# Windowed attention and a residual MLP on one core: copying three sets of transposes with one PSUM bank per engine, and three steps moved

## The chip, the cores and the metric

The kernel runs on one core of a Trainium2 chip. The metric is the time of one execution on the device in microseconds (us). The core's engines are TensorE (PE, with its weight loads listed apart as PEld), VectorE (DVE), ScalarE (ACT), GpSimd (POOL) and SyncE (SP); SP, ACT and POOL also issue DMAs. All times in this document are from profiled executions or from timed runs of the kernels shown.

## What is computed

Two parts, one after the other. First attention with a sliding window of 128 keys and 4 sink keys, for 4 batches, 8 heads, 768 positions, head size 64. Its heads side by side are the rows `x` (4 x 768 x 512) of a residual MLP that mixes first over positions and then over channels:

```python
scores = scale * np.matmul(q, k.transpose(0, 1, 3, 2))
scores = np.where(is_sink | in_window, scores, -1e9)
x = softmax(scores) @ v                       # heads side by side: B, S, 512
a1 = alpha1 * x + beta1
u  = x + lam * np.einsum('ts,bsd->btd', w_tok, a1)
a2 = alpha2 * u + beta2
out = u + lam * (np.maximum(a2 @ w_ch1, 0) @ w_ch2)   # 512 -> 2048 -> 512
```

## The kernel before

**Stages.** The four batches go through the stages below, one batch's MLP interleaved with the next batch's attention.

- q and k are cast to 16 bits and transposed on TensorE (`tp`, L505); scores are made for a block j of 128 keys and two groups of four heads (`S`, tiles `Sb_j_G`, L608), exponentials on ACT (`E`, L630), and masked by a multiplication on DVE (L645; on some blocks on POOL, L570). The sink keys have a small matmul of their own (`sk`, L540) and an exponential (`es`, L545). `pv` (L709) multiplies by v; DVE divides by the sums (L734, L735); POOL or DVE apply the first affine (`xh`, L753, L756).
- Token mixing: `tok` (L840), six matmuls of 128x512 for a block `ti` of 128 positions. DVE adds the result to x, which gives u (`ua`, L847), and ACT or POOL cast u to 16 bits (`u16`, L157 on POOL, L155 on ACT, both by the helper `copy`).
- u's transposes: for a half `chk` of 384 positions TensorE transposes three blocks `u16` of four groups of 128 channels (L881). Two channel groups go into one tile `uTp`, which is one bank of PSUM; so a set (a batch and a half) has two banks, `uTpb_chk_0` and `uTpb_chk_1`, with two channel groups each. Each channel group is copied to `uT` with the second affine by one instruction of 128x384, on ACT (L864) or on DVE (L866).
- First channel layer: `h` (L901), four matmuls of 128x384 for one of 16 channel blocks `fi` of a half, and a relu to `hT` on ACT (L907) or DVE (L909).
- Second channel layer: in batch 0 plain (`ch`, L1086, added to x by DVE at L1097); in batches 1 to 3 by Strassen's seven products `P1` to `P7` (`P`, L1018, eight matmuls of 128x256 for a block nt). P3 is added up in the bank of P5. Sums of w2 (`w2s`, and w2f in place, L933, on DVE or POOL) and of hT (L959 to L962) are made ahead. DVE adds the products to x (L1031) and into a side tile `pt` (L1049), and `pt` is added to x by DVE or POOL (L1054, L1057).

**Names.** `h1_0_13` is the tile h of batch 1, half 0, channel block 13; `tok1_5` the token mixing of batch 1, block 5; `u16_1_4` the cast of u of batch 1, block 4; `S2_1` the scores of batch 2, key block 1, both groups; `x3_5` the rows of batch 3, block 5; `P5_2_1` the product P5 of batch 2, nt 1.

**What sets the order.** Nothing is decided on the chip. The program makes 1153 tasks (a task is a few instructions of one engine), and a list written out by hand, `ORDER`, says in which order they are issued; the string `ENGINES` says which engine does each task, `HOMES` which buffer each tile takes. Each engine runs its own tasks in the order of that list. Between engines the framework adds semaphores. Four banks of PSUM hold all tiles of the kind "d" in turn (`tok`, `uTp`, `h`, `P`, `ch`, `pv`, `sk`, `tp`), so a tile's first matmul waits until the bank's former tile was read. The framework also makes two engines that touch one bank wait for each other: in the program's semaphores, an L866 on DVE waits for the L864 on ACT that reads the other half of the same bank, or the other way round.

**Around the change.** In batch 1's first set, each bank is copied by both engines; TensorE's order there is the two banks of transposes, four matmuls of `ch0_4`, `tok1_3` (in the bank of uTp1_0_1), `tok1_5` (in the bank of ch0_4), `tok1_4`, four matmuls of `pv2_0_0`, `h1_0_0`, `h1_0_2`, S2_1, then the second set's two banks, `h1_0_1`, `h1_0_13` (in the bank of uTp1_1_1), `h1_0_14` (in that of uTp1_1_0), `h1_0_15`. The copies of DVE stand among the subtraction of w2 (L933), the add of ch0_4 (L1097), the mask of E2_0_0 (L645) and the three adds of tok1_3, tok1_5 and tok1_4 (L847). The casts `u16_1_5` and `u16_1_4` are on POOL, `u16_1_3` on ACT. In batch 3, TensorE's order is tok3_5, P5_2_2, P3_2_0 (in the bank of P5_2_0), P5_2_1 (in the bank of tok3_5), the second set's banks uTp3_1_1 (in the bank of P5_2_0) and uTp3_1_0, P3_2_2, `h3_0_13` (in the bank of uTp3_1_1), `h3_0_1` (in the bank of uTp3_1_0), P3_2_1 (in the bank of P5_2_1), h3_0_12.

These lines issue a set's transposes and copies (`affine` holds L864 and L866):

```python
a = add(p, {PE: 336}, tr, [done["u16", b, 3 * chk + i] for i in range(3)], [pt] + us)
for ci in range(2):
    c = 2 * cp + ci
    done["uT", b, chk, c] = add(
        p + 0.1 + 0.01 * ci, {DVE: 395, ACT: 575},
        lambda e, ci=ci, c=c: affine(
            e, bo.t[:, c, chk * NTOK : (chk + 1) * NTOK], pt.t[:, ci, :], c),
        [a, done["ab2"]], [pt, bo])
```

Of the kernel before, what the change touches and what calls it, by code (L numbers as in the profile page):

```python
# [77 lines left out]
def kernel(  # L78
# [119 lines left out]
    for r in range(NR):  # L198
# [43 lines left out]
        451, 440, 452, 639, 453, 417, 319, 640, 309, 648, 446, 649, 320, 447, 418, 323, 321,  # L242
        448, 645, 664, 646, 324, 322, 449, 623, 329, 650, 665, 454, 347, 325, 651, 455, 330,
        652, 348, 326, 462, 456, 463, 464, 459, 656, 457, 327, 458, 659, 627, 460, 657, 662,
        625, 461, 331, 38, 629, 468, 356, 465, 470, 469, 332, 343, 466, 630, 467, 471, 660,
        333, 350, 622, 328, 310, 661, 658, 477, 884, 342, 883, 472, 474, 473, 889, 478, 479,
        671, 486, 475, 490, 476, 487, 344, 666, 491, 663, 483, 480, 484, 485, 488, 482, 481,
        672, 512, 489, 514, 513, 886, 669, 516, 515, 496, 667, 670, 506, 354, 497, 500, 517,
        507, 346, 510, 668, 684, 511, 881, 677, 685, 502, 678, 501, 682, 504, 683, 546, 505,
        686, 524, 503, 547, 334, 680, 520, 916, 525, 526, 687, 521, 628, 910, 544, 527, 631,  # L250
# [20 lines left out]
        807, 814, 990, 808, 841, 991, 987, 988, 839, 989, 842, 992, 845, 840, 843, 846, 822,  # L271
        847, 844, 993, 849, 836, 994, 850, 821, 997, 995, 848, 1000, 835, 998, 855, 1001,
        999, 851, 837, 996, 1002, 859, 838, 1012, 852, 856, 853, 860, 1006, 1013, 1009,
        1007, 1008, 1014, 1003, 863, 1004, 1005, 854, 1015, 1010, 864, 1011, 857, 872, 862,
        869, 1016, 873, 1017, 866, 870, 861, 1021, 1018, 1022, 1023, 878, 858, 1019, 1020,
        1050, 867, 879, 1026, 875, 1027, 1051, 1048, 876, 1030, 1049, 1038, 1031, 1042,
        1039, 1028, 1043, 1034, 1029, 1044, 1052, 1045, 1035, 1046, 1086, 1047, 1053, 1080,
        1087, 1084, 874, 1081, 1064, 1085, 1032, 1065, 1070, 1033, 1068, 1071, 1058, 1024,
# [11 lines left out]
        "4444433134433334413334413314444042210221021021020121321021320202020020211212020202020212"  # L290
        "1212020212120202120212120212121202020202022221022221422221022221422221022221013111111331"
        "1111333333302002002132132002032002102020101212010321213120301212131201012121312010121213"
        "1203212131212131213213210201201210213213201201212020202120202121212020202021212020212121"
        "2120211120202120202020201120212121212111112121212121212113211121312142102142142142104444"
        "0000444044333333020020320020020020020020020201012120101212133201012121312030121213120101"
        "2121332032121312121312102102102012012102102102012012121212021212121212120212120202120212"
        "1202020202011212020202021202011202121212121111121212121212121312111213121021421421021421"
        "4044440440440443333330200200200200203200203200202010121203012121312010121213320103212131"
        "2030121213120321213321213121021021020120121021321320120120202120212021212021202020202021"
        "2020212120202020112020212021202020112120210202142141111212121212121211121112131210210214"  # L300
        "214214210"
    )
# [993 lines left out]
```

## Time and profile before

| | us |
|---|---|
| median of 3 runs (267.78 to 268.67) | 268.48 |
| the profiled execution | 268.26 |
| its span, first to last instruction | 266.3 |
| PE busy | 257.6 |
| DVE busy | 196.0 |
| ACT busy | 140.0 |
| POOL busy | 113.2 |

The granted TensorE clock is full in every slice of the page. The span is the profiled execution without what lies before the first and after the last instruction. Matmuls are pipelined, and a row of the timeline gives the start and the length until the modelled end of the last one, which can lie past the start of the next row. In a row of the timeline the brackets hold the engine's idle time before it and what ended that time.

### The profile page before, as it was taken

The numbers are of one execution on the slowest core, as the hardware profiler recorded it, in microseconds if no ns is written. First come the engines' busy times: TensorE is split into PE (matmuls) and PEld (weight loads), VectorE is DVE, ScalarE is ACT, GpSimd is POOL, SyncE is SP. The second block draws the span as 40 slices with busy tenths as digits, with TensorE's granted clock in tenths as the row PEclk, the third lists the DMA queues.
The fourth block names the chain that finished last, engine by engine and source line by source line (L and its number), as shares of the span: only waits on it lengthen the run. The fifth ranks groups of instructions, "written<-read, shape, count | busy, mean of one in ns | idle before, by whom it ended". The sixth has DMA issues, their size and how long they took to land.

```text
span 266.3 us, 5785 instructions
## 1 busy us (share of the span) xinstructions
PE 257.6 (97%) x2335; PEld 170.8 (64%) x2335; DVE 196.0 (74%) x403; ACT 140.0 (53%) x227; POOL 113.2 (43%) x131
## 2 busy tenths in 40 slices
PE   8999999999999999999999999999999999999993
PEld 8755556675556544565787776667667666667882
DVE  5789898679787748687877976588688974128892
ACT  1389744799967434669773452752760324543000
POOL 7826906979974437134763030064563120000010
PEclk9999999999999999999999999999999999999999
DMA  7999999999186307637430007010000000100217
GB/s 214 212 273 326 231 249 354 369 268 315 44 214 206 79 0 190 186 100 196 86 118 2 0 0 238 2 42 0 2 0 2 0 2 0 39 2 1 98 68 269
DMA packets 43058, 33.30 MB, mean 125 GB/s; under 512 B 26372, under 2 KB 37388, under 8 KB 43032
## 3 DMA queue, kind: packets, MB, share of 16 engines
q1 hardware_dynamic: 31728, 23.34, 29.6%
q10 hardware_dynamic: 7560, 6.32, 7.8%
q0 software_dynamic: 3744, 3.28, 7.7%
q8 instruction: 18, 0.29, 0.5%
q14 instruction: 8, 0.07, 0.1%
HBM read 29.91 MB, written 6.29 MB: 136 GB/s over the span
## 4 chain that ended last, share of the span: by engine, by line
PE 81%; DVE 8%; ACT 5%; DMA 2%; issue 1%; SPq 0%; DVEq 0%; ACTq 0%
PE h L901 29%; PE P L1018 19%; PE tok L840 9%; PE ch L1086 8%; PE pv L709 3%; PE tp L505 3%; PE S L608 3%; PE idle L148 3%; DMA nat<-in_q_dram 2%; ACT uT L864 2%; DVE uT L866 1%; ACT E L630 1%; PE uTp L881 1%; DVE qkT L157 1%; DVE x L735 1%
## 5 line engine op out<-in xcount | busy, mean ns | idle before, releaser
L901 PE MATMUL h<-uT,w1f 128*128 128x384 f16 x512 | 90.4, 326 | 1.1 <-DVE uT L866 0.5
L901 PEld LDWEIGHTS <-w1f 128*128 128x128 f16 x512 | 48.0, 98 | 32.8 <-issue 3.6
L907 ACT ACTIVATE hT<-h 128x384 f16<-128x384 f32 x77 | 36.2, 492 | 35.1 <-PE h L901 29.5
L909 DVE TENSOR_SCALAR hT<-h 128x384 f16<-128x384 f32 x51 | 27.8, 554 | 22.0 <-PE h L901 19.6
L1018 PEld LDWEIGHTS <-hT 128*128 128x128 f16 x408 | 39.3, 98 | 7.3 <-issue 1.0
L630 ACT ACTIVATE E<-S 128x1024 f16<-128x1024 f32 (+1 forms) x39 | 38.2, 1002 | 6.4 <-PE S L608 4.9
L753 POOL TENSOR_TENSOR tm<-x,la_b 128x512 f32<-128x512 f32 x18 | 24.4, 1358 | 28.1 <-DVE x L735 14.7
L840 PE MATMUL tok<-xh,wtokT 128*128 128x512 f16 x144 | 33.3, 379 | 0.3 <-DVE x L1097 0.2
L1018 PE MATMUL P<-w2f,hT 128*128 128x256 f16 x216 | 26.9, 273 | 0.0
L155 ACT COPY qkT<-tp 128x768 f16<-128x768 f16 x24 | 19.0, 800 | 11.8 <-PE tp L505 11.1
L1031 DVE TENSOR_TENSOR x<-x,P 128x256 f32<-128x256 f32 x45 | 18.2, 418 | 9.2 <-PE P L1018 8.8
L1018 PE MATMUL P<-w2s,hT 128*128 128x256 f16 x192 | 23.7, 273 | 0.5 <-DVE x L847 0.4
L155 ACT CAST u<-x 128x512 f16<-128x512 f32 x16 | 9.6, 618 | 27.7 <-DVE x L847 27.3
L840 PEld LDWEIGHTS <-wtokT 128*128 128x128 f16 x144 | 13.8, 97 | 15.5 <-issue 1.1
L1086 PE MATMUL ch<-w2f,hT 128*128 128x512 f16 x96 | 23.4, 380 | 0.0
L1054 POOL TENSOR_TENSOR x<-x,pt 128x256 f32<-128x256 f32 x4 | 3.4, 853 | 46.5 <-DVE pt L1049 46.5
L735 DVE TENSOR_TENSOR x<-pv,rec 128x256 f32<-128x256 f32 x48 | 20.4, 425 | 1.7
L847 DVE TENSOR_TENSOR x<-x,tok 128x512 f32<-128x512 f32 x24 | 16.0, 682 | 4.4 <-PE tok L840 4.1
L709 PEld LDWEIGHTS <-E 128*128 128x128 f16 x328 | 14.9, 97 | 4.9 <-issue 1.1
L709 PE MATMUL pv<-vfs,E 128*128 128x65 f16 x328 | 17.6, 194 | 0.0
L822 POOL TENSOR_TENSOR w2f<-wst_w,lam_b 128x512 f16<-128x512 f32 x12 | 16.9, 1431 | 0.0
L864 ACT ACTIVATE uT<-uTp,ab 128x384 f16<-128x384 f16 x16 | 10.2, 668 | 11.8 <-PE uTp L881 9.7
(131 smaller groups left out, 376.0 us busy)
## 6 DMA issues: line engine op xcount, KB each, us to landing
wst_w<-in_moe_w_ch_dram SPq DMA_DIRECT2D x8, 512.0 KB, 7.1
nat<-in_q_dram SPq DMA_DIRECT2D x10, 384.0 KB, 6.9
nat<-in_k_dram SPq DMA_DIRECT2D x10, 384.0 KB, 5.6
vnat<-in_v_dram SPq DMA_DIRECT2D x14, 256.0 KB, 4.7
out_dram<-x SPq DMA_DIRECT2D x11, 256.0 KB, 2.4
out_dram<-x ACTq DMA_DIRECT2D x10, 256.0 KB, 2.1
wtn<-in_moe_w_tok_dram SPq DMA_DIRECT2D x6, 384.0 KB, 5.9
w1f<-in_moe_w_ch_dram POOLq DMA_DIRECT2D x4, 512.0 KB, 10.5
```

The lines of the kernel that those rows point to most:

```text
L155: nc.scalar.copy(o, i)
L630: nc.scalar.activation(eT.t, pS.t[:, :, 0 : n * w].rearrange("p e (i w) -> p e i w", i=n), AF.Exp, scale=scale)
L709: nc.tensor.matmul(po.t[:, hl, :], eT.t[:, e_, off + i, c : c + P], vf[j][:, h, :], start=(r < 2 and n == 0), stop=(n == len(parts) - 1 an ...
L735: nc.vector.tensor_mul(bx.t[:, 4 * G : 4 * G + 4, :], po.t[:, :, 0:D], rec.t.to_broadcast([P, 4, D]))
L753: engine[e].tensor_mul(bt.t, bx.t.rearrange("p h d -> p (h d)"), la1_b)
L840: nc.tensor.matmul(pt.t, wtokT[:, si, ti * P : (ti + 1) * P], hs[si].t, start=(si == 0), stop=(si == NR - 1))
L901: nc.tensor.matmul(ph.t, w1f[:, c, fi * P : (fi + 1) * P], bu.t[:, c, chk * NTOK : (chk + 1) * NTOK], start=(c == 0), stop=(c == NC - 1))
L907: nc.scalar.activation(bh.t[:, fi, :], ph.t, AF.Relu)
L909: nc.vector.tensor_scalar_max(bh.t[:, fi, :], ph.t, 0.0)
L1018: nc.tensor.matmul(pc.t, hh[:, nt * P : (nt + 1) * P], w(fi), start=(first and n_ == 0), stop=(n_ == HF - 1), skip_group_check=True)
L1031: nc.vector.tensor_add(row(bx)[:, cols], row(bx)[:, cols], pc.t)
L1086: nc.tensor.matmul(pc.t, bh.t[:, fi, nt * P : (nt + 1) * P], w2f[:, fi, :], start=(fi == 0), stop=(fi == NF - 1))
```

## The change

The order of the tasks and the engines of four of them are changed; no instruction is added or taken away, and no tile gets another buffer.

- Engines: in batch 1's first set, both copies of bank uTp1_0_1 are DVE's and both of uTp1_0_0 ACT's (before: one of each on each engine). In batch 1's second set, uTp1_1_1 is ACT's and uTp1_1_0 DVE's. In batch 3's second set, uTp3_1_1 is DVE's and uTp3_1_0 ACT's. Each engine has as many copies as before.
- Task 666, the scores S2_1 on TensorE, moves from before the transposes of batch 1's second set to behind them and behind h1_0_1.
- Task 1016, the add L847 of x3_5 on DVE, moves ahead of task 862, the add L1057 of x2_5.
- Task 333, the add L1097 of x0_4 on DVE, moves ahead of task 467 (a copy that was DVE's and is now ACT's) and of 471 (tok1_3).

```diff
-        625, 461, 331, 38, 629, 468, 356, 465, 470, 469, 332, 343, 466, 630, 467, 471, 660,
-        333, 350, 622, 328, 310, 661, 658, 477, 884, 342, 883, 472, 474, 473, 889, 478, 479,
-        671, 486, 475, 490, 476, 487, 344, 666, 491, 663, 483, 480, 484, 485, 488, 482, 481,
+        625, 461, 331, 38, 629, 468, 356, 465, 470, 469, 332, 343, 466, 630, 333, 467, 471,
+        660, 350, 622, 328, 310, 661, 658, 477, 884, 342, 883, 472, 474, 473, 889, 478, 479,
+        671, 486, 475, 490, 476, 487, 344, 491, 663, 483, 480, 484, 485, 488, 666, 482, 481,
...
-        1007, 1008, 1014, 1003, 863, 1004, 1005, 854, 1015, 1010, 864, 1011, 857, 872, 862,
-        869, 1016, 873, 1017, 866, 870, 861, 1021, 1018, 1022, 1023, 878, 858, 1019, 1020,
+        1007, 1008, 1014, 1003, 863, 1004, 1005, 854, 1015, 1010, 864, 1011, 857, 872, 1016,
+        862, 869, 873, 1017, 866, 870, 861, 1021, 1018, 1022, 1023, 878, 858, 1019, 1020,
...
-        "1203212131212131213213210201201210213213201201212020202120202121212020202021212020212121"
+        "1203212131212131213213210200211210213213211200212020202120202121212020202021212020212121"
...
-        "2030121213120321213321213121021021020120121021321320120120202120212021212021202020202021"
+        "2030121213120321213321213121021021020120121021321320021120202120212021212021202020202021"
```

In `ENGINES` a 0 is ACT, 1 DVE, 2 PE, 3 POOL, 4 SP; each task has its digit.

## The prediction

> **What bounds the kernel now.** I read the page first, then the list of waits, then the timelines of the two stretches that the diff touches. From the page, the busy times and the chain that ended last (a line of shares by engine):
>
> ```profile
> PE 257.6 (97%) x2335; PEld 170.8 (64%) x2335; DVE 196.0 (74%) x403; ACT 140.0 (53%) x227; POOL 113.2 (43%) x131
> PE 81%; DVE 8%; ACT 5%; DMA 2%; issue 1%; SPq 0%; DVEq 0%; ACTq 0%
> ```
>
> TensorE bounds it. No step of the diff takes a matmul away, so only TensorE's idle moments can be won. From the list of waits (total, times, longest):
>
> ```profile
> DVE uT L866 <- ACT uT L864: 5.8, 8, 1.5
> ACT uT L864 <- DVE uT L866: 2.1, 2, 1.1
> PE h L901 <- DVE uT L866: 0.5, 2, 0.3
> ```
>
> The two copies of one bank (L864 on ACT, L866 on DVE) wait for each other although they read different halves; TensorE then waits for the later one, because its next tile is that bank. First stretch, A (batch 1; start, length): TensorE, then the others.
>
> ```profile
> 101.64 1.46 PE L840 MATMUL tok<-xh,wtokT 128*128 128x512 f16 x6
> 103.31 2.75 PE L840 MATMUL tok<-xh,wtokT 128*128 128x512 f16 x12 [0.21 <-DVE x L1097]
> 107.42 0.61 PE L608 MATMUL S<-qkT 64*128 64x256 f16 x8
> 107.96 0.84 PE L881 MATMUL uTp<-iden,u 128*128 128x128 f16 x12
> 109.74 0.81 PE L901 MATMUL h<-uT,w1f 128*128 128x384 f16 x4 [0.29 <-DVE uT L866]
> 110.83 1.46 PE L901 MATMUL h<-uT,w1f 128*128 128x384 f16 x8 [0.28 <-ACT uT L864]
> ```
> ```profile
> 102.18 0.48 DVE L866 TENSOR_SCALAR uT<-uTp,ab 128x384 f16<-128x384 f16 x1 [0.64 <-ACT uT L864]
> 102.58 0.68 DVE L1097 TENSOR_TENSOR x<-x,ch 128x512 f32<-128x512 f32 x1
> 103.17 1.62 DVE L645 TENSOR_TENSOR E<-E,mask 128x1024 f16<-128x1024 f16 x1
> ```
> ```profile
> 101.98 2.26 POOL L933 TENSOR_TENSOR w2f<-w2f 128x512 f16<-128x512 f16 x2
> 106.91 0.61 POOL L157 CAST u<-x 128x512 f16<-128x512 f32 x1 [0.19 <-DVE x L847]
> ```
>
> Second stretch, C (batch 3), TensorE and DVE:
>
> ```profile
> 218.57 1.03 PE L1018 MATMUL P<-w2s,hT 128*128 128x256 f16 x8 [0.42 <-DVE x L847]
> 219.44 0.83 PE L881 MATMUL uTp<-iden,u 128*128 128x128 f16 x12
> 221.21 0.81 PE L901 MATMUL h<-uT,w1f 128*128 128x384 f16 x4
> 222.20 0.81 PE L901 MATMUL h<-uT,w1f 128*128 128x384 f16 x4 [0.18 <-DVE uT L866]
> ```
>
> The bracketed idle is short of the loss, since a matmul's modelled end overlaps the next start. I count by starts: 4 h matmuls pass in 0.65 us back to back (108.64 is followed at 109.74, so 0.45 is lost), 8 P in 0.87, 6 tok in 1.30, 12 transposes in 0.67, 8 S in 0.54.
>
> **Step 1, batch 1's first set (A).** ACT and DVE each keep two copies; only the pairing changes. Two copies by one engine take 0.86 on DVE (109.21) and 1.23 on ACT (219.98). DVE then holds uTp1_0_1 from 100.41 to 101.28 and no longer waits until 102.18 for ACT. Its subtraction L933 follows (0.75 beside POOL, to about 101.95; 102.1 if POOL's cast gets in first), then the add L1097, starting between 101.6 and 102.0 and done between 102.3 and 102.7 instead of at 103.25. TensorE: tok1_3 needs DVE's copies (101.33), and TensorE is free at 101.40: start 101.40, not 101.64. tok1_5 needs L1097: 102.70, not 103.31. tok1_4 at 104.00, h1_0_0 at 105.43, 0.6 earlier. The ends of ACT's work here hardly move: two copies from 100.74 to 101.96, the exponential to 102.86.
>
> **The mask after it.** This decides how much more comes. It took 1.62 where the median of its form is 0.68, beside POOL's two subtractions (to 103.13 and 104.24). [...] The exponential now lets the mask start at 102.89, inside POOL's first subtraction: by that row it ends at 103.12 + 0.55 = 103.67, not 104.79. If it comes after 103.1 it stays at 104.79. I take 103.67, margin 0.2.
>
> **Step 2, S2_1 moved behind the transposes; batch 1's second set (A).** With the mask at 103.67, u16_1_4 is bounded by tok1_4 (done 105.46): add 105.49 to 106.18, POOL's cast (0.13 later, 0.61 long) to 106.93. TensorE finishes h1_0_2 at 106.72 and formerly had the 0.54 of S2_1 before the transposes; that cover is gone, so it idles for some 0.2 with its whole queue behind that wait, and the transposes start at about 106.9. They pass until 107.58; h1_0_1 to 108.23; S2_1 covers the copies to 108.77. ACT's pair (from 107.45) ends at 108.69, DVE's earlier: h1_0_13 and h1_0_14 no longer wait, and h1_0_15 starts at 110.08 instead of 111.48. S2_1's exponentials, its only readers, formerly began at 111.42, after a relu that still stands before them; nobody is late by the move. **A gives 1.40.** With the mask at 104.79, POOL's cast ends at 107.34, the transposes start at 107.4, and h1_0_15 at 110.6: 0.88.
>
> **Step 3, x3_5's add before L1057 (C).** It runs 217.24 to 217.92 instead of 217.84 to 218.52. TensorE is free at 217.99: P5_2_1 starts there, 0.57 earlier. DVE's sum until 219.18 is the same, and the transposes' first bank is freed by its last member (L1031 of x2_0, 219.18): they start at 219.23 instead of 219.44. So 0.21 is left. What queues behind the exchange: L1057 and two adds L1031, with no one waiting sooner. [...]
>
> **Step 4, batch 3's second set (C).** DVE's pair: 219.77 to 220.64; P3_2_2 at 219.90; h3_0_13 at 220.77 (TensorE's own pace) instead of 221.21; ACT's pair 220.11 to 221.34; h3_0_1 at 221.42 instead of 222.20; L1031 of x2_4 is done at 221.57, in time for P3_2_1 at 222.07. **C gives 0.78.** ACT and DVE reading different banks at once cost nothing in the trace: 220.55 and 220.69 overlap at 0.67 and 0.48.
>
> **At no cost.** L1097's move (task 333) passes only a step that went to ACT and one of TensorE's; no order of a queue changes by it. POOL's and SP's order is unchanged. After 104 us no idle time of a compute engine ends with a DMA, so loads don't cap the gain.
>
> **Sum:** 1.40 + 0.78 = 2.18. The profiled execution took 268.26 (span 266.3 and 1.96 around it): 266.08. The median of the runs is 0.22 above it: **266.3**.
>
> **Rivals.**
> R1, the mask misses its place: 0.88 + 0.78 = 1.66, 266.8. For it: the margin of 0.2. Against: only POOL being early could cause it. Chance 0.2.
> R2, slower: DVE starves while POOL has work queued. Then L933 at 101.2 waits for POOL's cast and both subtractions to 104.24; L1097 ends at 105.1, tok1_5 starts at 105.15 instead of 103.31, and the transposes, now without S2_1 before them, wait for a u16_1_4 at about 109.4: h1_0_15 at 112.6, 1.1 lost. In C L1057 waits for POOL's cast and add to 219.4, L1031 of x2_0 ends at 220.6, h3_0_1 starts at 222.8, 0.6 lost: 270.2. It decides once u16_1_4 is later than 108.25 (A's break-even) by more than C's 0.78. [...] Chance 0.08.
> R3, the gain of A isn't kept: DVE, 77% busy from 112 to 190, becomes the bound before batch 2's softmax ends, and 0.78 or less is left: 267.7, on the border of what can be told. For it: TensorE waits for DVE at 190 to 193. Against: DVE idles for 17 us in those 78, mostly waiting for TensorE. That the copies are not on the path at all would end here too. Chance 0.17.
>
> **Numbers.** Forecast 0.55 (266.3), R1 0.2, R3 0.17, R2 0.08. About 0.3% (0.8 us) is what a measurement of this kernel can tell from no change. Faster by over that: 0.78 (the forecast, R1 and a little of R3); within: 0.15 (the rest of R3, and R2 in a mild form); slower: 0.07. The range reaches from 265.6 (the forecast, with 0.7 for the spread of the runs and A's other stalls) to 267.9 (R3 and its spread).
>
> **What would show it.** Right: no wait between L864 and L866 in A and at 220; the mask L645 near 103 at 1.0 or less; transposes near 107; h1_0_15 near 110.1 and h3_0_1 some 2.2 early. Wrong: the mask still at 1.6; TensorE idle before the transposes L881 by more than 0.7; TensorE idle for DVE near 190 longer than before; a longer L1057 or a late u16_3_5 in C.

## The result, and the profile after

| | before | after |
|---|---|---|
| median of 4 runs, us (lowest to highest) | 268.13 (267.68 to 268.67) | 265.76 (265.74 to 266.04) |
| the profiled execution | 268.26 | 265.74 |
| its span | 266.3 | 263.9 |

The ratio is 0.9919, interval 0.9903 to 0.9936: the time is 0.5 us below the forecast, 266.3, and inside its range. Timed again, the change gave 266.32 against 268.13 (6 and 11 runs), ratio 0.9935 (0.9916 to 0.9954). In the executions that have a trace, 0.5 us of the first difference is luck at the start of the program, which is taken out below: the change itself is worth 1.87 us.

The page after; busy times, the chain that ended last, and the group of h's matmuls:

```profile
PE 256.3 (97%) x2335; PEld 170.5 (65%) x2335; DVE 195.1 (74%) x403; ACT 140.1 (53%) x227; POOL 114.0 (43%) x131
PE 86%; ACT 6%; DVE 5%; issue 1%; DVEq 0%; ACTq 0%
L901 PE MATMUL h<-uT,w1f 128*128 128x384 f16 x512 | 90.1, 326 | 0.3 <-DVE x L847 0.2
```

The same work is done. TensorE's share of the chain is 86% here and was 81% before, but second executions of the two kernels read 84% and 78%, and DVE's share 3% and 4%, so these shares vary too much between executions to carry the argument. The h matmuls have 0.3 us of idle time before them in all, and in the list of waits no wait of theirs for a copy (L864 or L866) is left. Two lines of that list (total, times, longest):

```profile
DVE uT L866 <- ACT uT L864: 2.8, 5, 1.2
PE uTp L881 <- DVE x L1031: 0.4, 1, 0.4
```

DVE's wait for the other engine's half of a bank was 5.8 in 8; what is left belongs to sets that the change doesn't touch. The wait of ACT for DVE has gone from the list. The second line is new: in C the transposes now wait for the add that frees their bank. The forecast has this wait, but 0.19 shorter; the experiments show why.

Batch 1 after, TensorE (start, length, engine, line, what, count, idle time before):

```profile
99.32 0.83 PE L881 MATMUL uTp<-iden,u 128*128 128x128 f16 x12
99.98 1.03 PE L1086 MATMUL ch<-w2f,hT 128*128 128x512 f16 x4
100.85 4.05 PE L840 MATMUL tok<-xh,wtokT 128*128 128x512 f16 x18
...
106.32 0.89 PE L881 MATMUL uTp<-iden,u 128*128 128x128 f16 x12
107.05 0.81 PE L901 MATMUL h<-uT,w1f 128*128 128x384 f16 x4
107.79 0.61 PE L608 MATMUL S<-qkT 64*128 64x256 f16 x8
108.34 2.45 PE L901 MATMUL h<-uT,w1f 128*128 128x384 f16 x14
```

The 18 tok matmuls are one row without a gap: tok1_5 no longer waits for L1097. h1_0_13, h1_0_14 and what follows are one row too, where before each waited 0.3 for a copy. DVE and POOL beside it:

```profile
99.85 0.86 DVE L866 TENSOR_SCALAR uT<-uTp,ab 128x384 f16<-128x384 f16 x2 [1.49 <-PE uTp L881]
100.63 0.41 DVE L933 TENSOR_TENSOR w2s<-w2f,w2s 128x512 f16<-128x512 f16 x1
101.05 0.69 DVE L1097 TENSOR_TENSOR x<-x,ch 128x512 f32<-128x512 f32 x1
102.37 0.81 DVE L645 TENSOR_TENSOR E<-E,mask 128x1024 f16<-128x1024 f16 x1 [0.63 <-ACT E L630]
```
```profile
101.48 2.71 POOL L933 TENSOR_TENSOR w2f<-w2f 128x512 f16<-128x512 f16 x2
...
105.75 0.61 POOL L157 CAST u<-x 128x512 f16<-128x512 f32 x1 [0.64 <-DVE x L847]
```

DVE's two copies are one row of 0.86, as forecast. The mask takes 0.81 instead of 1.62, and POOL's two subtractions 2.71 instead of 2.26: the second one, which starts while the mask runs, takes 1.60 where the first takes 1.15. Nobody waits for it. The last cast of the set, u16_1_4, ends at 106.36; the transposes start at 106.32, and the second of them, which reads that cast, at 106.42: TensorE meets POOL there, and S2_1 is no longer in between. Batch 3 after, TensorE and then DVE:

```profile
217.58 0.83 PE L881 MATMUL uTp<-iden,u 128*128 128x128 f16 x12 [0.40 <-DVE x L1031]
218.25 1.04 PE L1018 MATMUL P<-w2f,hT 128*128 128x256 f16 x8
219.12 1.46 PE L901 MATMUL h<-uT,w1f 128*128 128x384 f16 x8
```
```profile
215.40 0.68 DVE L847 TENSOR_TENSOR x<-x,tok 128x512 f32<-128x512 f32 x1
216.00 0.68 DVE L1057 TENSOR_TENSOR x<-x,pt 128x512 f32<-128x512 f32 x1
216.78 0.75 DVE L1031 TENSOR_TENSOR x<-x,P 128x256 f32<-128x256 f32 x2
218.12 0.86 DVE L866 TENSOR_SCALAR uT<-uTp,ab 128x384 f16<-128x384 f16 x2 [0.59 <-PE uTp L881]
```

The same steps of DVE in before:

```profile
217.24 0.69 DVE L1057 TENSOR_TENSOR x<-x,pt 128x512 f32<-128x512 f32 x1
217.84 0.68 DVE L847 TENSOR_TENSOR x<-x,tok 128x512 f32<-128x512 f32 x1
218.44 0.75 DVE L1031 TENSOR_TENSOR x<-x,P 128x256 f32<-128x256 f32 x2
```

h3_0_13 and h3_0_1 are one row of eight without a wait. The transposes wait 0.40 for the L1031 row (the adds of x2_5 and of x2_0), and that row begins 0.78 after L1057, though L1057 is 0.68 long. In before, each of these steps begins 0.60 after the one ahead of it.

**Taking the start out.** All that stands ahead of 97 us is the same in both programs, yet batch 1's first transposes (uTp1_0_1) begin at 99.87 before and at 99.32 after. TensorE's first row, 67 matmuls that only keep it busy, in before, in after, and in a second profiled execution of before:

```profile
1.06 6.74 PE L148 MATMUL idle<-warm 128*128 128x128 f16 x67 [1.06 <-DVE warm L174]
```
```profile
1.06 6.24 PE L148 MATMUL idle<-warm 128*128 128x128 f16 x67 [1.06 <-DVE warm L174]
```
```profile
1.06 5.19 PE L148 MATMUL idle<-warm 128*128 128x128 f16 x67 [1.06 <-DVE warm L174]
```

The same 67 matmuls take 6.74, 6.24 and 5.19 us, so it differs from one execution to the next. In the first two traces 0.5 of the 2.4 us between the spans is there already. I therefore measure from the start of uTp1_0_1 to the end of the span: 166.46 before, and 166.48 in the second execution of before. The table gives, from that same mark, by how much the start of each tile (and the end) is earlier than in before, in us; it is worked out from the starts in the traces.

| kernel | tok1_5 | uTp1_1_1 | h1_0_15 | tok3_5 | P5_2_1 | uTp3_1_1 | h3_0_13 | h3_0_1 | end |
|---|---|---|---|---|---|---|---|---|---|
| before_again | -0.01 | -0.01 | -0.01 | 0.00 | -0.01 | -0.01 | -0.01 | -0.01 | -0.01 |
| after | 0.62 | 1.09 | 1.28 | 1.29 | 1.87 | 1.31 | 1.54 | 1.88 | 1.87 |
| after_again | 0.61 | 1.09 | 1.28 | 1.29 | 1.87 | 1.30 | 1.53 | 1.87 | 1.87 |
| e1_set1 | 0.61 | 0.61 | 0.61 | 0.61 | 0.60 | 0.60 | 0.60 | 0.60 | 0.60 |
| e2_set2 | 0.00 | 0.48 | 0.67 | 0.68 | 0.67 | 0.67 | 0.67 | 0.67 | 0.68 |
| e4_s21_alone | 0.00 | 0.48 | 0.43 | 0.45 | 0.44 | 0.44 | 0.44 | 0.44 | 0.44 |
| e3_c | 0.00 | 0.00 | 0.00 | 0.00 | 0.58 | 0.00 | 0.23 | 0.57 | 0.56 |
| e5_x35_alone | 0.00 | 0.00 | 0.00 | 0.02 | 0.59 | 0.02 | 0.02 | 0.03 | 0.02 |
| e6_set3_alone | 0.00 | 0.00 | -0.01 | -0.01 | -0.02 | -0.02 | 0.21 | 0.55 | 0.54 |
| e7_late_mask | 0.61 | 0.80 | 0.81 | 0.81 | 1.39 | 0.82 | 1.05 | 1.39 | 1.39 |
| e8_x20_first | 0.61 | 1.09 | 1.28 | 1.28 | 1.86 | 1.81 | 2.00 | 2.34 | 2.33 |
| e9_x20_before_l1057 | 0.61 | 1.09 | 1.28 | 1.29 | 1.87 | 1.87 | 1.84 | 2.18 | 2.18 |

Read along a row: A has given 1.28 by h1_0_15, and the same 1.29 still stands at tok3_5, 100 us later; C adds 0.59. Two executions of one program agree to 0.02 here, while their starts of uTp1_0_1 differ by a quarter of a us (99.87 and 100.12, 99.32 and 99.56). Where two programs are the same up to a tile, the table shows up to 0.02 as well, so 0.02 counts as nothing.

### The profile page after: what moved, and what is told of

Read it like the earlier page. It is cut to its first block, busy times and chain, and to the rows that moved or that the text cites. A ratio compares the mean times of both kernels' runs of the same rounds, so it can differ in the third digit from the quotient of the medians.

```text
span 263.9 us, 5785 instructions
## 1 busy us (share of the span) xinstructions
PE 256.3 (97%) x2335; PEld 170.5 (65%) x2335; DVE 195.1 (74%) x403; ACT 140.1 (53%) x227; POOL 114.0 (43%) x131
## 4 chain that ended last, share of the span: by engine, by line
PE 86%; ACT 6%; DVE 5%; issue 1%; DVEq 0%; ACTq 0%
PE h L901 31%; PE P L1018 19%; PE tok L840 11%; PE ch L1086 8%; PE S L608 3%; PE pv L709 3%; PE tp L505 3%; PE idle L148 2%; ACT E L630 2%; PE uTp L881 2%; ACT wt L805 1%; ACT uT L864 1%; DVE qkT L157 1%; DVE x L847 1%; DVE uT L866 1%
## 5 line engine op out<-in xcount | busy, mean ns | idle before, releaser
L1031 DVE TENSOR_TENSOR x<-x,P 128x256 f32<-128x256 f32 x45 | 18.2, 418 | 9.4 <-PE P L1018 8.9
L847 DVE TENSOR_TENSOR x<-x,tok 128x512 f32<-128x512 f32 x24 | 16.0, 681 | 4.9 <-PE tok L840 4.7
L864 ACT ACTIVATE uT<-uTp,ab 128x384 f16<-128x384 f16 x16 | 10.1, 667 | 10.5 <-PE uTp L881 10.5
```

The lines of the kernel that those rows point to most:

```text
L847: nc.vector.tensor_add(xf, xf, pt.t)
```

## The experiments

The theory is that of the prediction: a bank shared by ACT and DVE makes TensorE wait for the later copy, and the moves let the gain through. Against it stood that the gain belongs to the moves and not to the pairing, that the mask decides it (R1), and that it is lost downstream (R3). In the diffs below, ORDER shows only the stretch that is changed, and ENGINES a task's digit (0 ACT, 1 DVE).

### The kernel before, again, as the measure

> The kernel before once more, nothing changed. In the profile of before the 67 idle matmuls at the start took 6.74 us, in that of after 6.24, and all that follows stands 0.5 us earlier there. Theory (that half microsecond is luck of the start and no work of the change): the start differs again from run to run, between 6.2 and 6.8, and the span from the first transposes of q (L505) on is 258.3 as before. Rival (the change brings the early start): 6.74 again.

Measured: 268.04 against 268.09, ratio 0.9998 (0.9982 to 1.0013), 10 and 31 runs. From the mark to the end it is the first execution of before within 0.02. The expectation missed twice: the idle row took 5.19, less than 6.2, and from the first transposes of all (L505) on, which began at 7.00 instead of 7.95, the span is 259.6 and not 258.3. So the luck of the start isn't over with the idle row; behind the mark of the table it is.

### Set 1 alone

```diff
-ORDER    466, 630, 467, 471, 660, 333, 350
+ORDER    466, 630, 333, 467, 471, 660, 350
-ENGINES  467: 1, 469: 0
+ENGINES  467: 0, 469: 1
```

> Only batch 1's first set with one bank per engine (tasks 467 and 469, and 333 moved). Theory: the mask of E2_0_0 starts inside POOL's first subtraction and takes about 0.8 instead of 1.62; tok1_5 and h1_0_0 start 0.6 earlier, and that stays: 0.6 us less from the first transposes of q on, about 267.5 against 268.1. Rival (the bank wait is not on the path): no change.

Measured: 267.92, ratio 0.9992 (0.9977 to 1.0008), which by itself tells nothing (0.60 would be a ratio of 0.9978); by the marks 0.60, all of it there at tok1_5 and unchanged to the end. The mask took 0.81, as expected. Task 333 passes 467, 471 and 660, none of them DVE's, so it is the pairing alone that is tried here. This is step 1 without the mask's part: with S2_1 still ahead of the transposes, an earlier u16_1_4 brings no more.

### S2_1 and set 2; S2_1 alone

```diff
-ORDER    487, 344, 666, 491, 663, 483, 480, 484, 485, 488, 482
+ORDER    487, 344, 491, 663, 483, 480, 484, 485, 488, 666, 482
-ENGINES  481: 0, 485: 1
+ENGINES  481: 1, 485: 0
```

> Only batch 1's second set with one bank per engine (tasks 481 and 485) and S2_1 (666) behind it. Theory: the mask stays at 1.6, POOL's cast of u16_1_4 ends where it did; the transposes start 0.4 earlier after a stall of 0.7, the two waits of 0.45 between h1_0_1 and h1_0_15 are gone: 0.7 us less. Rival (the cover that S2_1 gave is worth as much as the waits): no change or slower.

Measured: 267.62, ratio 0.998 (0.9965 to 0.9996); 0.68 by the marks. The stall of 0.7 ahead of the transposes didn't come: by starts TensorE stands 0.16 there (h1_0_0 at 105.47, the transposes at 106.93, and the two h between them take 1.30). Then the same without the two digits:

```diff
-ORDER    487, 344, 666, 491, 663, 483, 480, 484, 485, 488, 482
+ORDER    487, 344, 491, 663, 483, 480, 484, 485, 488, 666, 482
```

> The engines as before; only S2_1 (666) moved behind the transposes and h1_0_1. From batch 1's first set of transposes on, against before: theory (two things add up, S2_1 covers the copies and the pairing shortens them): the transposes start 0.48 earlier, h1_0_15 about 0.4 earlier, and 0.4 us stay to the end. Rival (the pairing alone gives the gain of the second set, the move is only an exchange of one cover for another): 0.

Measured: 267.91 against 267.77 (one run each, too few to tell); 0.44 by the marks. ACT's copies in this kernel:

```profile
108.25 0.67 ACT L864 ACTIVATE uT<-uTp,ab 128x384 f16<-128x384 f16 x1
109.86 0.67 ACT L864 ACTIVATE uT<-uTp,ab 128x384 f16<-128x384 f16 x1 [0.93 <-DVE uT L866]
```

The second copy still stands 0.93 behind DVE's use of the bank and ends at 110.53, and h1_0_14 starts at 110.58, 0.90 after h1_0_13 instead of 0.65. In the kernel with the digits changed too, the same two tiles start 0.66 apart. So S2_1's place brings 0.44 and the pairing 0.24 on top; the pairing without the move wasn't run. Most of what the two copies cost each other is covered by S2_1 once S2_1 stands behind the transposes.

### Batch 3: both parts, and each alone

```diff
-ORDER    857, 872, 862, 869, 1016, 873
+ORDER    857, 872, 1016, 862, 869, 873
-ENGINES  1020: 1, 1022: 0
+ENGINES  1020: 0, 1022: 1
```

> Only batch 3's part: its second set with one bank per engine (1020, 1022) and x3_5's add (1016) ahead of L1057. Theory after the result: 0.6 us less, since L1057 and the add L1031 of x2_5 that reads what it wrote now stand side by side on DVE, with 0.18 between their starts more than before. Rival (the prediction as written, DVE's sum unchanged): 0.78 less.

Measured: 267.24, ratio 0.9976 (0.9961 to 0.999); 0.56 by the marks, where 0.78 was forecast. The exchange on DVE alone (the ORDER lines):

> Only x3_5's add (1016) ahead of L1057, engines as before. Theory: P5_2_1 starts 0.57 earlier, but the transposes wait for the add of x2_0, which DVE ends when it did: 0.0 at the transposes and at the end. Rival (the prediction as written): 0.2 less.

Measured: 267.70 against 267.77, one run each; 0.02 by the marks, which is nothing. Its DVE:

```profile
216.77 0.69 DVE L847 TENSOR_TENSOR x<-x,tok 128x512 f32<-128x512 f32 x1
217.37 0.69 DVE L1057 TENSOR_TENSOR x<-x,pt 128x512 f32<-128x512 f32 x1
218.16 0.75 DVE L1031 TENSOR_TENSOR x<-x,P 128x256 f32<-128x256 f32 x2
```

The add L847 is earlier, and P5_2_1 with it (0.59). But L847 formerly stood between L1057 and the first L1031, and both of these write x2_5. Now they are neighbours: L1057 follows L847 after 0.60, the first L1031 follows L1057 after 0.79. The second L1031, which frees the transposes' bank, ends as late as before, and P5_2_1's early start turns into idle time ahead of the transposes. The pair alone (the ENGINES lines):

> Only batch 3's second set with one bank per engine (1020, 1022). Theory: the whole 0.57 of batch 3's part, h3_0_13 0.23 earlier and h3_0_1 0.57. Rival (the pair and the exchange need each other): 0.3 or less.

Measured: 267.63 against 267.77, one run each; 0.54 by the marks. Its TensorE:

```profile
218.60 1.03 PE L1018 MATMUL P<-w2s,hT 128*128 128x256 f16 x8 [0.42 <-DVE x L847]
219.47 0.83 PE L881 MATMUL uTp<-iden,u 128*128 128x128 f16 x12
220.14 1.04 PE L1018 MATMUL P<-w2f,hT 128*128 128x256 f16 x8
221.01 1.46 PE L901 MATMUL h<-uT,w1f 128*128 128x384 f16 x8
```

P5_2_1 keeps its old wait for the add of x3_5, and h3_0_13 and h3_0_1 are yet one row: all of C comes from the pair. 0.54 and 0.02 make the 0.56 of both.

The three parts add up: 0.60 + 0.68 + 0.56 = 1.84, against 1.87 for the whole change.

### The mask put late

The rival R1, made on purpose: ACT does a sink exponential (task 658) ahead of E2_0_0's, so that the mask becomes ready only in POOL's second subtraction. The rest is the changed kernel.

```diff
-ORDER    467, 471, 660, 350, 622, 328, 310, 661, 658, 477
+ORDER    467, 471, 658, 660, 350, 622, 328, 310, 661, 477
```

> The changed kernel with ACT's small exponential es2 ahead of that of E2_0_0 (658 ahead of 660), so that the mask can start only 0.5 later, after POOL's first subtraction. Theory (first come, and the whole instruction): the mask is caught by the second subtraction and takes 1.4 or more, u16_1_4 ends about 1 us later, the transposes of batch 1's second set start 0.4 to 0.5 later than in the changed kernel: 0.4 to 0.5 us more at the end. Rival (the mask has slack): 0.

Measured: 266.80 against 267.77, one run each; 1.39 by the marks, 0.48 less than the whole change. Its DVE and POOL:

```profile
103.43 1.44 DVE L645 TENSOR_TENSOR E<-E,mask 128x1024 f16<-128x1024 f16 x1 [1.11 <-ACT E L630]
```
```profile
102.06 2.26 POOL L933 TENSOR_TENSOR w2f<-w2f 128x512 f16<-128x512 f16 x2
```

POOL's second subtraction ends at 102.06 + 2.26 = 104.32, the mask at 104.87: 0.55 later, the same distance as in before (104.24 and 104.79), and the mask, which starts at 103.43 inside that subtraction, takes 1.44. tok1_5 has its 0.61 here too; the loss comes after the mask, at h1_0_0 (0.39 instead of 0.61), at the transposes (0.80 instead of 1.09) and within their row, which waits for POOL's casts and takes 1.07 instead of 0.89.

### The changed kernel again, and the adjacency undone

> The changed kernel once more. Theory (all of the gain lies behind the start-up, 1.87 us in the profile, and the rest of the first difference of 2.4 was the luck of the start): 1.6 to 2.2 us under the kernel before, ratio 0.992 to 0.994, with runs spread over about a microsecond as those of before are. Rival (the change shortens the start too): 0.991 or less.

Measured: 266.32, ratio 0.9935 (0.9916 to 0.9954); the marks are those of the first run. If neighbours that write one x cost the 0.2 that C lacks, then one add between them returns it. The L1031 of x2_0, the very add that frees the transposes' bank, was put ahead of that of x2_5:

```diff
-ORDER    872, 1016, 862, 869, 873, 1017, 866, 870, 861
+ORDER    872, 1016, 862, 869, 870, 873, 1017, 866, 861
```

> The changed kernel with the add L1031 of x2_0 (870) ahead of that of x2_5 (873), so that the transposes' bank is freed first and L1057 is not followed by the add that reads its result. Theory: x2_0's add starts 0.5 earlier, the transposes of batch 3's second set 0.4 earlier, bounded then by POOL's cast of u16_3_5; 0.4 us less at the end than the changed kernel. Rival (the transposes wait for the cast anyway): 0.

Measured: 265.96, ratio 0.9919 (0.9901 to 0.9937); 2.33 by the marks, 0.46 better than the change. Its DVE, and TensorE's transposes:

```profile
215.55 0.68 DVE L847 TENSOR_TENSOR x<-x,tok 128x512 f32<-128x512 f32 x1
216.15 0.69 DVE L1057 TENSOR_TENSOR x<-x,pt 128x512 f32<-128x512 f32 x1
216.75 0.75 DVE L1031 TENSOR_TENSOR x<-x,P 128x256 f32<-128x256 f32 x2
```
```profile
217.22 0.88 PE L881 MATMUL uTp<-iden,u 128*128 128x128 f16 x12
```

The L1031 that follows L1057 is now another x's and follows after 0.60; and the bank is free one L1031 (0.33) earlier. 0.18 + 0.33 = 0.51; the transposes gained 0.50 of it and are left with a wait of 0.05 (P5_2_1, ahead of them, begins at 216.30 and takes 0.87). One step further, the same add ahead of L1057 as well:

```diff
-ORDER    872, 1016, 862, 869, 870, 873, 1017
+ORDER    872, 1016, 869, 870, 862, 873, 1017
```

> As the one before, with L1057 of x2_5 (862) behind x2_0's add too: x3_5, x2_0, L1057, x2_5 on DVE. Theory: POOL's cast of u16_3_5 no longer meets L1057 and takes 0.61 instead of 0.94; the transposes start at TensorE's own pace, 0.55 earlier than in the changed kernel; but the add of x2_5 ends later and holds P3_2_2: 0.3 to 0.4 less at the end. Rival (no wait at P3_2_2): 0.55.

Measured: 266.65, ratio 0.9937 (0.9921 to 0.9954); 2.18 by the marks. The transposes come 0.06 earlier still, at TensorE's own pace, and POOL's cast takes 0.61 again, as expected. But x2_0's add now stands 0.34 waiting for its product from TensorE, so L1057 and the add of x2_5, which frees the bank of P3_2_2, come later: h3_0_13 has 1.84 where the version above has 2.00. That version, with x2_0's add just behind L1057, is the best one found; by the runs alone it can't be told from the change (265.96 and 266.32, overlapping intervals), by the marks it can.

## Why the prediction was right, and where it was off

The forecast was faster, by steps that each had a place and a price. By the marks the sum was 1.87 where 2.18 was forecast; the first two traces differ by 2.4 only because 0.5 of start-up luck lies on top. That the second timing, 266.32, meets the forecast of 266.3 is luck too: the forecast starts from a median of 268.48 for the kernel before, of three runs, where later runs give 268.13 and 268.09, and this 0.35 makes up for the 0.31 that the gain lacks.

- **Set 1's pairing, 0.6:** right, 0.60 alone. DVE's pair took its 0.86, L933 got in ahead of POOL's cast and took 0.41 (0.75 in the forecast, which changes nothing: the add L1097 then starts as its product is ready), and tok1_3 and tok1_5 came 0.24 and 0.62 earlier (forecast 0.24 and 0.61).
- **The mask:** right. The forecast's 103.67 stands on 0.55 between the end of the POOL instruction in which a mask begins and the mask's own end. In before the masks that begin at 62.58, 193.56 and 103.17 take 1.29, 1.11 and 1.62, and end at 63.86, 194.68 and 104.79; the POOL instructions in which they begin end at 63.31, 194.13 and 104.24. In after the first subtraction ended at 102.63 and the mask at 103.18, again 0.55. So the mask began inside POOL's first subtraction and took 0.81. With both traces put on the same mark (0.55 added to after's times) it ended at 103.73, forecast 103.67. The late mask shows that the choice between 103.67 and 104.79 was real, and its price: 0.48, forecast 0.52. Without set 1's gain the mask costs nothing: in the run with S2_1 and set 2 alone it still takes 1.62, and yet DVE stands 0.11 waiting for TensorE ahead of tok1_4's add.
- **S2_1 and set 2:** right in kind, short by 0.12. On the same mark the transposes started at 106.87 (forecast 106.9), but h1_0_15 at 110.20 (forecast 110.08). The mis-sized term is S2_1: I counted 0.54 for it between two h, as it took ahead of the transposes. Between two h, S2_1 starts 0.74 after h1_0_1 and h1_0_13 0.55 after S2_1; less the 0.65 that h1_0_1 would take anyway, that is 0.64. The trace of before had the row: there too S2_1 began 0.75 after an h (106.67 and 107.42). The other 0.05 is the transposes' row, 0.73 by starts instead of 0.67, since its second matmul met POOL's cast; the row began 0.03 ahead of the forecast. So A was 1.28, not 1.40.
- **Step 3, x3_5's add ahead of L1057:** wrong in the sentence "DVE's sum until 219.18 is the same". It is 0.19 longer: from x3_5's add to the L1031 of x2_0 1.72 pass (215.40 to 217.12), where the same three steps took 1.53 before (217.24 to 218.77). The move took away what stood between two adds of which the second reads and writes the x that the first wrote; the second then starts only after the first has ended (216.67 and 216.78), while an independent one starts 0.08 before. I asked who waits for the steps that are moved, not what they had hidden. So the transposes got 0.02, not 0.21, and C was 0.59, not 0.78.
- **POOL's cast against L1057:** L1057 was first (216.00, the cast at 216.21) and kept its 0.68; the cast took 0.94 instead of 0.61 and ended at 217.15, ahead of the transposes at 217.58.
- **Set 3's pairing:** right; it forecast 0.78 - 0.21 = 0.57 and gave 0.54 alone.
- **No cap downstream (R3) and no starving (R2):** A's 1.28 at h1_0_15 is 1.29 at tok3_5, so nothing between 112 and 190 us took any of it. DVE never waited for more than one POOL instruction in these stretches: the mask ended at 103.18 while POOL's second subtraction ran on to 104.19, and L1057 kept its 0.68 beside the cast. No run shows the longer waits of which R2 is made up.

**What stays open.** Why the neighbours cost 0.18 in one place and less elsewhere: the L1031 of x2_4 also follows the L1057 of x2_4, at 218.90 and 219.61 in the changed kernel, 0.71 apart; and so it is for x2_5 in the last experiment (0.71). The longer 0.78 stands where POOL's cast begins beside L1057, but the cast isn't needed for it. Before has the same distance, 0.79, near its end, where POOL's last instruction ended at 258.59:

```profile
258.94 0.68 DVE L1057 TENSOR_TENSOR x<-x,pt 128x512 f32<-128x512 f32 x1
259.73 0.42 DVE L1031 TENSOR_TENSOR x<-x,P 128x256 f32<-128x256 f32 x1
```

Nor is it a late product of TensorE: in the changed kernel the semaphore of that product came at 216.33, that of L1057 at 216.69, and L1031 began at 216.78. What the traces show is the number of semaphores. The adds at 0.78 and 0.79 wait for two, DVE's own and TensorE's; those at 0.71 for DVE's alone. Over the 13 traces, DVE instructions that were released by an earlier one of DVE start 22 to 24 ns after its semaphore where that is the only one (632 times; in before and in after one more starts 40 ns after); with two, either 22 to 24 or 91 to 94 ns after (148 times). What decides between these two isn't shown. What sets the start of the program was not separated either: the idle row explains 0.50 of the 0.55 between the first two traces, but the second execution of before had the fastest idle row of the three and reached uTp1_0_1 last.

## What to carry to other kernels

Where two engines read one bank of PSUM and are made to wait for each other, give each engine a bank of its own: the copies cost the same here (one L864 668 ns before and 667 after, one L866 474 and 474), and it was worth 0.60 and 0.54 us for two of the sets, and 0.24 for the one whose wait S2_1 already covers in part. Before a step is moved on a busy engine, ask what it stood between, and which step behind it frees a buffer; here, putting that one first was worth 0.46, and the move itself nothing (0.02). To tell tenths of a us apart, measure from a mark behind the start of the program, not from the first instruction.

## What was not expected of the hardware

The 67 idle matmuls begin with starts 107 ns apart and go over to 56 ns, after 25 to 55 of them, from one execution to the next: at 3.8 us of the span in the second execution of before, at 7.0 in the first. The first execution (window, its length, TensorE busy and matmuls, granted clock, then DMA), and the second:

```profile
3.00:5.00 2.00, 2.00 (x22) 1.00 1.01 295
```
```profile
3.00:5.00 2.00, 2.00 (x32) 1.00 1.04 354
```

22 against 32 matmuls of one shape in 2 us. The granted clock of 1.00 in these rows is no evidence of a full clock there: in the first execution the trace's records of the clock begin only at 7.02 us and in the second at 3.78, and a time without a record counts as full in the views, also in the first slices of the page's PEclk. In all 13 executions traced here the first record, at 1.00, begins within 0.04 us of the change of spacing. What makes the spacing change isn't shown; in the 13 executions the change lies between 2.7 and 6.0 us behind the first matmul. The start of uTp1_0_1 lies between 99.32 and 100.86.

Two adds on DVE of which the second reads what the first wrote, an L1057 and an L1031, start 0.71 to 0.79 apart in these traces (218.90 and 219.61 in after, 258.94 and 259.73 in before); where an add of another x follows an L1057, it starts 0.60 after (216.15 and 216.75 with x2_0's add first).
